# A three-stage mLSTM, mixture-of-experts and PReLU kernel: branch tables around whole experts replaced by straight code over 256 slots and one branch for the rest

## The chip, the cores and the metric

One NeuronCore of a Trainium2 chip runs the whole program. The metric is the device time of one execution in microseconds; lower is better.

## The reference

What is computed, cut to the steps that matter here (the recurrent first stage is left as a call):

```python
x = mlstm(q, k, v, i_gate, f_gate, o_gate)            # 1536 tokens x 320
logits = x @ w_gate                                   # 8 experts
expert_idx = np.argmax(logits, axis=1)
...
for i in range(N):                                    # first come, first served, 384 slots an expert
    e = expert_idx[i]
    if counts[e] < capacity:
        disp[e, counts[e]] = x[i]
...
h = np.maximum(np.einsum('ecd,edf->ecf', disp, w1), 0.0)   # 320 -> 1024
y = np.einsum('ecf,efd->ecd', h, w2)                       # 1024 -> 320
out[i] = gate_w[i] * y[expert_idx[i], pos[i]]
...
h = out @ w_in                                        # 320 -> 2048
g = np.maximum(h, 0.0) + alpha * np.minimum(h, 0.0)
return g @ w_out                                      # 2048 -> 320
```

How many tokens an expert gets depends on the data. With the seeded inputs the counts of experts 0 to 7 are 250, 143, 283, 182, 88, 227, 58 and 305.

## The kernel before, in words

**Three stages.** The mLSTM stage works through 12 blocks of 128 tokens, routes them and scatters each token's row into its expert's slots in DRAM (`disp`, 384 slots an expert). The expert stage takes the eight experts one after the other. The last stage (PReLU) gathers the tokens' rows back in groups of 2, 4, 4 and 2 blocks of 128 and runs 320 -> 2048 -> 320 over each group.

**Numbers as two halves.** Every matmul operand is a pair, high and low part in fp32r. ScalarE (ACT) copies a value to its high part, and VectorE (DVE) or GpSimd (POOL) subtracts the high part to get the low one (`less`, L183). A product is three matmuls: high by high, high by low, low by high. The inner dimension 320 is two blocks of 128 rows and one of 64; for the block of 64 the weight tile holds the high rows in its upper half and the low rows in its lower half, so that two matmuls do: one of 128 rows against the high part of x stored twice, and one of 64 rows against the low part of x (`layer1`, L926 to L937). One `layer1` call is eight matmuls. `layer2` (L944) is three matmuls of 320 columns for each block of 128 slots.

**An expert.** Its hidden dimension of 1024 is taken in eight steps f of 128. Step f does `layer1`, then the relu and its two parts (ACT L1082, DVE L1083), then `layer2` for step f - 2 (`LAG`). Beside it the weights of the next expert are split, a quarter (two steps) at a time, by `split1` and `split2`: the high parts on ACT, the low part of `w2` on POOL, that of `w1` on DVE except for the last quarter, which is POOL's; the next expert's rows are transposed and split (`expert_x`); and a piece of the last stage's float64 weights is converted on DVE with its parts on ACT and POOL (`split_f64`, five operations a piece; `CUT` says how many in each expert). Split weights live in a ring of six quarters (`ring1`, `ring2`), raw quarters in one set of buffers (`raw1`, `raw2`) that is loaded anew for each expert.

**The branch.** Each expert is emitted once for each number of slots (128, 256, 320 or 384) and for each number of blocks of the next expert: twelve arms, four for the last. `values_load` (L1163) reads the arm's number from `armi` into a register of PE, ACT, DVE and POOL, and `tc.Switch` (L1180) jumps into the arm; at its end each engine jumps back. With the counts above the slots computed are 256, 256, 320, 256, 128, 256, 128 and 320. SyncE (SP) issues the DMAs and takes no part in the switch.

**Order.** The instructions of PE, ACT, DVE and POOL stay in the order in which the code is written; SP's order is the scheduler's. The loads of expert e + 1 (`load_quarter`) stand ahead of the switch of expert e.

Of the kernel before, what the change touches and what calls it, by code (L numbers as in the profile page):

```python
# [53 lines left out]
def kernel(  # L54
# [39 lines left out]
    ARMS = [n for n in (P, 2 * P, 5 * P // 2) if n < SL] + [SL]  # L94

    W1, W2, W6, V7, V8, V9, G0, G1, NA, WA, WB, Z0, Z1, X0, LD, FL, XE, SC, SC0, L0, F0, WC, LS, UO, DL, LOV, XG, XG2, LV, L9, E0, S0, CUT, PQ = 12, 4, 0, 0, (1, 2, 1, 4, 1, 2, 0, 4, 2, 2, 2, 2, 1, 2, 4, 1), (1, 3, 4, 6), 2, 11, 6, 0, 6, 3, 6, 3, 3, (2, 1, 2, 4, 1), 5, (0, 1, 0, 1, 0, 1, 0, 3), (0, 0, 0, 0, 2, 0, 0, 1), 3, {5:[0], 6:[1], 7:[2]}, 0, 1, 1, 4, (12, ), (9, 11, 13), (11, 12, 13), 3, 3, 2, 0, (5, 5, 10, 5, 5, 5, 5, 20), ((3, ), (3, ))
# [39 lines left out]
    def x_tiles(pool, n, i):  # L136
        return [[pool.tile([P, n], F32R, name=f"x{i}{k}{x}", bufs=1) for x in "hl"] for k in range(3)]
# [4 lines left out]
    RING = 6  # L142
# [30 lines left out]
    def load_quarter(e, q, anchor=None):  # L173
        ds = [nc.sync.dma_start(out=raw_quarter(q)[:, :2], in_=w1[e, q])]
        if q % 2 == 0:
            ds.append(nc.sync.dma_start(out=raw1[q // 2][:r, 2, :], in_=w1t[e, :, q * QF:(q + 2) * QF]))
        ds.append(nc.sync.dma_start(out=raw2[q], in_=w2[e, :, 2 * q:2 * q + 2, :]))
        for d in ds:
            if anchor is not None:
                after(d, anchor)  # L180
# [42 lines left out]
    with ExitStack() as actx:  # L223
# [659 lines left out]
        arm, blks = (cp.tile([P, E], F32, name=nm) for nm in ("arm", "blks"))  # L883
        for t, ns in ((blks, range(P, SL, P)), (arm, ARMS[:-1])):
            for n in ns:
                if n == ns[0]:
                    nc.vector.tensor_single_scalar(out=t, in_=cps, scalar=float(n), op=ALU.is_gt)
                else:
                    nc.vector.scalar_tensor_tensor(out=t, in0=cps, scalar=float(n), in1=t, op0=ALU.is_gt, op1=ALU.add)
        nc.vector.scalar_tensor_tensor(  # L890
            out=arm[:, :E - 1], in0=blks[:, 1:], scalar=float(len(ARMS)), in1=arm[:, :E - 1], op0=ALU.mult, op1=ALU.add,
        )
# [33 lines left out]
    def layer1(ps, wh, wl, xp, fs, ks=(0, 2, 1)):  # L926

        n = ps.shape[-1]
        seq = []
        for k in ks:  # L930
            hi, lo = (t[:, :n] for t in xp[k])
# [21 lines left out]
    NRAW = 3  # L953
# [55 lines left out]
    def out_parts(q):  # L1009

        at = lambda i: (NQ * E + i) % RING
        if q in (2, 3):
            return [view(t, 2, DM) for t in ring1[at(q - 2)]]
        return ring2[at(q if q < 2 else q - 2)]
# [23 lines left out]
    ghl = [[mp.tile([P, SL], F32R, name=f"g{x}{i}") for x in "hl"] for i in range(LAG + 1)]  # L1038
# [9 lines left out]
    def expert_x(e, k, nblk):  # L1048
        x_part(lambda m: xd[:, m, :], nblk, lambda k: xps[k % 2], xp2[e % 2], k)
# [4 lines left out]
    def expert(e, n, nxt):  # L1054

        nblk = -(-n // P)

        def second(f, ms=range(nblk)):
            h2, l2 = ring2[(NQ * e + f // 2) % RING]
            gh, gl = (t[:, :n] for t in ghl[f % (LAG + 1)])  # L1060
            layer2([(m, accs[m]) for m in ms], gh, gl, h2[:, f % 2, :], l2[:, f % 2, :], f == 0, f == NF - 1)

        more = e + 1 < E
        shifts[:] = over
# [6 lines left out]
        per = len(steps) // NF  # L1071
        for f in range(NF):
            q, fo = divmod(f, 2)
            bank = lambda f: hps[f % (3 if more else 2)][:, :n]
            ps = bank(f)
            l1 = lambda f: (bank(f), *first_parts(e, f // 2), xp2[e % 2], slice(f % 2 * P, (f % 2 + 1) * P))
            if e or f >= E0:
                layer1(*l1(f))
            elif f == 0:
                first_layers([l1(f) for f in range(E0)])  # L1080
            gh, gl = (t[:, :n] for t in ghl[f % (LAG + 1)])
            nc.scalar.activation(gh, ps, AF.Relu)  # L1082
            nc.vector.scalar_tensor_tensor(out=gl, in0=ps, scalar=0.0, in1=gh.bitcast(F32), op0=ALU.max, op1=ALU.subtract)  # L1083
            x0 = X0 if e == 0 else XE
            if more and x0 <= f < x0 + 3:
                expert_x(e + 1, f - x0, nxt)
# [5 lines left out]
            if f >= LAG:  # L1092
                second(f - LAG)
# [4 lines left out]
            if more:  # L1098
                (split2 if fo else split1)(e + 1, q, nc.vector if not fo and q not in (PQ[1] if n > P else PQ[0]) else nc.gpsimd)
# [5 lines left out]
        for f in range(NF - LAG, NF if more else 0):  # L1105
            second(f)
        if more:
            while steps:
                steps.pop(0)()
            for m in range(nblk):  # L1110
                copy = nc.scalar.copy if m % 2 else nc.vector.tensor_copy
                p = min(P, n - m * P)
                copy(ysb[:p, m, :], accs[m][:p, :DM])
            return

        def put(m):
            p = min(P, n - m * P)
            for k in range(3):
                for a in range(2):
                    x = yhl[m][:p, a, k * P:min((k + 1) * P, DM)]  # L1120
                    nc.tensor.matmul(
                        fx[k][:x.shape[-1]], x, spot[:p, m, :GB0 * P], start=False, stop=m == nblk - 1 and a == 1,
                    )

        for m in range(nblk):
            for f in range(NF - LAG, NF):
                second(f, [m])
            p = min(P, n - m * P)
            hi, lo = (yhl[m][:p, a] for a in range(2))
            nc.scalar.copy(hi, accs[m][:p, :DM])  # L1130
            less(lo, accs[m][:p, :DM], hi, nc.vector)
            nc.gpsimd.tensor_tensor(out=ysb[:p, m, :], in0=hi.bitcast(F32), in1=lo.bitcast(F32), op=ALU.add)
        for m in range(nblk):
            put(m)
        while steps:
            steps.pop(0)()

# [4 lines left out]
    y_out = []  # L1142
# [7 lines left out]
    low_rows()  # L1150
    for e in range(E):
        if e == 3:
            last_steps()
        if e + 1 < E:
            x_in = load_x(e + 1)
            for q in range(NQ):
                load_quarter(e + 1, q, x_first if e == 0 else None)
        done = sum(CUT[:e]) // 5
        while loaded < min(done + NRAW, LD + done if e == 0 else 99):
            load_conv(loaded, x_in if e == 0 else None)  # L1160
            loaded += 1
        arms = len(ARMS) * (NBLK if e + 1 < E else 1)
        arm = nc.values_load(  # L1163
            armi[0:1, e:e + 1], engines=engines, min_val=0, max_val=arms - 1,
            skip_runtime_bounds_check_because="a count of comparisons",
        )
        over = list(shifts)
        if e == E - 2:
            nc.vector.tensor_copy(first_slots, gidx[:, :GB0].unsqueeze(2).to_broadcast([P, GB0, P]))
        if e == E - 1:  # L1170
            raw1 = raw2 = None
            yhl = [rw.tile([P, 2, DM], F32R, tag=f"w2r{m}", name=f"yhl{m}") for m in range(NBLK)]
            load_conv(loaded, raw=rw.tile([P, 3 * QF * 2], U32, tag="w1r1", name="raw"))
            loaded += 1
            spot = rw.tile([P, 3, 2 * QF], F32R, tag="w1r0", name="spot")
            nc.gpsimd.memset(xd[:, :GB0, :], 0.0)
# [58 lines left out]
    for gi, (i0, nb) in enumerate(PARTS):  # L1235
# [3 lines left out]
        for f in range(NFF):  # L1239
# [25 lines left out]
            def l2step(i0=i0, nb=nb, f=f, gh=gh, gl=gl, accs=accs):  # L1265
# [5 lines left out]
                if f == NFF - 1:  # L1271
                    osb = sp.tile([P, GB, DM], F32, tag="osb", name="osb", bufs=1)
                    for m in range(nb):
                        i = i0 + m

                        if m % 2:
                            nc.scalar.activation(osb[:, m, :], accs[m][:, :DM], AF.Copy, scale=gwt[:, i:i + 1])  # L1277
                        else:
                            nc.vector.tensor_scalar_mul(osb[:, m, :], accs[m][:, :DM], gwt[:, i:i + 1])
                        nc.sync.dma_start(out=out[i * P:(i + 1) * P, :], in_=osb[:, m, :])  # L1280
# [84 lines left out]
```

## Time and profile before

| what | value |
|---|---|
| median of 3 runs | 586.05 us (573.05 to 588.75) |
| profiled execution, its own time | 577.92 us |
| its span, first to last instruction | 576.1 us |
| mean granted TensorE clock | 0.855 of 2.4 GHz |
| PE busy, share of the span | 510.4 us, 89% |
| DVE, ACT, POOL busy | 299.6, 236.1, 224.5 us |

The stages follow one another: the mLSTM stage to about 126 us, the experts to about 366, the last stage to the end. Busy time is an average over stages with different limits; what an edit is worth is read from its own stage. A granted clock of 0.50 means 1.2 GHz, 1.00 means 2.4 GHz.

### The profile page before, as it was taken

The page shows a single profiled execution, that of the slowest core. Times are in us where ns is not written, and L with a number is a line of the kernel's source. Part 1 is how long each engine was busy: PE and PEld are TensorE (multiplying, and loading weights), DVE is VectorE, ACT ScalarE, POOL GpSimd, SP SyncE. Part 2 cuts the span into 40 slices and gives each one's busy share as a digit, 9 for nine tenths or more (in the row PEclk, how much of TensorE's full clock was granted, in tenths as well). Part 3 has the DMA queues.
Part 4 walks back from the last instruction along what each step waited for, and adds up shares of the span by engine and source line. Part 5 has one row for each costly group of instructions (what it writes and reads, how often), then busy time and mean ns, then how long its engine had stood idle before and what let it go on. Part 6 is the DMA issues. An engine that isn't in the chain of part 4 may idle for free. (4 is left out here: it accounts for less than half of the span.)

```text
span 576.1 us, 7915 instructions
## 1 busy us (share of the span) xinstructions
PE 510.4 (89%) x2699; PEld 425.5 (74%) x2699; DVE 299.6 (52%) x606; ACT 236.1 (41%) x563; POOL 224.5 (39%) x194
## 2 busy tenths in 40 slices
PE   7789988888787896969696969999999999999997
PEld 3578867866676674859575958788777877778886
DVE  8457636776748393927192639699221322122222
ACT  3467743343433242424242322355443434434443
POOL 3253344563423241414251442476453334232331
PEclk8779877576969896965595579999999999999999
DMA  7999994238956445454545053230010002000100
GB/s 216 271 281 334 324 279 159 68 105 245 246 148 178 128 140 173 141 166 134 173 132 176 0 153 92 85 92 0 24 46 1 1 0 71 0 1 1 47 1 23
DMA packets 41128, 69.91 MB, mean 121 GB/s; under 512 B 3999, under 2 KB 29922, under 8 KB 40975
## 3 DMA queue, kind: packets, MB, share of 16 engines
q1 hardware_dynamic: 39615, 64.18, 37.7%
q0 software_dynamic: 1152, 3.86, 2.1%
q8 instruction: 46, 0.75, 0.6%
q14 instruction: 107, 0.88, 0.6%
q10 hardware_dynamic: 208, 0.24, 0.1%
HBM read 56.49 MB, written 11.85 MB: 119 GB/s over the span
## 5 line engine op out<-in xcount | busy, mean ns | idle before, releaser
L183 POOL TENSOR_TENSOR g3l<-g,g3h 128x512 fp32r<-128x512 f32 (+1 forms) x61 | 66.7, 1094 | 112.4 <-ACT g3h L1258 112.3
L1255 DVE SCALAR_TENSOR_TENSOR g<-ng,nalt,g 128x256 f32<-128x256 f32 (+1 forms) x64 | 43.2, 675 | 124.8 <-ACT g L1254 122.9
L183 POOL TENSOR_TENSOR w2l<-w2r,w2h 128x640 fp32r<-128x640 f32 x31 | 53.4, 1721 | 116.8 <-ACT w2h L215 57.8
L1253 ACT ACTIVATE ng<-hps 128x256 f32<-128x256 f32 (+1 forms) x64 | 31.5, 493 | 102.8 <-PE hps L937 100.1
L1082 ACT ACTIVATE gh<-hps 128x256 fp32r<-128x256 f32 (+2 forms) x50 | 18.8, 375 | 116.5 <-PE qs L937 56.1
L1083 DVE SCALAR_TENSOR_TENSOR gl<-hps,gh 128x256 fp32r<-128x256 f32 (+2 forms) x50 | 20.4, 408 | 76.4 <-ACT gh L1082 72.9
L949 PE MATMUL acc<-w2h,gh 128*128 128x320 f32 (+1 forms) x128 | 46.0, 360 | 1.7 <-ACT gh L1082 1.7
L951 PE MATMUL acc<-w2h,gl 128*128 128x320 f32 (+1 forms) x128 | 43.6, 341 | 3.1 <-DVE gl L1083 3.1
L950 PE MATMUL acc<-w2l,g3h 128*128 128x320 f32 x144 | 44.5, 309 | 0.0
L951 PE MATMUL acc<-w2h,g3l 128*128 128x320 f32 x144 | 44.5, 309 | 0.0
L949 PE MATMUL acc<-w2h,g3h 128*128 128x320 f32 x144 | 44.4, 308 | 0.0
L950 PE MATMUL acc<-w2l,gh 128*128 128x320 f32 (+1 forms) x128 | 42.7, 334 | 0.0
L378 ACT ACTIVATE Gb<-Gb,bT 128x128 f32<-128x128 f32 x96 | 29.6, 390 | 14.0 <-POOL Gb L370 14.0
L1258 ACT CAST g3h<-g 128x256 fp32r<-128x256 f32 (+1 forms) x64 | 32.9, 515 | 0.3 <-DVE g L1255 0.3
L1254 ACT ACTIVATE g<-hps 128x256 f32<-128x256 f32 (+1 forms) x64 | 31.1, 486 | 1.6 <-POOL g3l L183 1.3
L384 PE MATMUL qs<-qbd,qk 120*128 120x384 f32 (+1 forms) x72 | 30.7, 573 | 0.4 <-DVE Pt L400 0.3
L951 PEld LDWEIGHTS acc<-w2h,gl 128*128 128x128 f32 (+1 forms) x128 | 26.0, 203 | 5.4 <-DVE gl L1083 5.2
L949 PEld LDWEIGHTS acc<-w2h,gh 128*128 128x128 f32 (+1 forms) x128 | 26.5, 207 | 2.5 <-ACT gh L1082 2.2
L949 PEld LDWEIGHTS acc<-w2h,g3h 128*128 128x128 f32 x144 | 27.1, 188 | 1.1
L950 PEld LDWEIGHTS acc<-w2l,g3h 128*128 128x128 f32 x144 | 27.0, 188 | 1.0
L447 PEld LDWEIGHTS Ops<-tk,Pt 128*128 128x128 f32 x192 | 26.4, 215 | 1.4 <-DVE Um L434 0.9
L937 PE MATMUL hps<-x10h,w1h 128*128 128x256 f32 (+1 forms) x26 | 9.5, 364 | 20.0 <-issue 19.3
(306 smaller groups left out, 1399.5 us busy)
## 6 DMA issues: line engine op xcount, KB each, us to landing
w2r<-w SPq DMA_DIRECT2D x32, 320.0 KB
w1r<-w SPq DMA_DIRECT2D x32, 256.0 KB
Gb<-gd SPq DMA_DIRECT2D x12, 512.0 KB
raw<-wout SPq DMA_DIRECT2D x8, 640.0 KB
raw<-win SPq DMA_DIRECT2D x8, 512.0 KB
tk<-tok SPq DMA_DIRECT2D x6, 648.0 KB
disp<-zt SPq DMA_DIRECT2D x4, 960.0 KB
yd<-held_rows SPq DMA_DIRECT2D x8, 480.0 KB
```

What stands on the lines that cost most here:

```text
L183: eng.tensor_tensor(out=out, in0=a, in1=b.bitcast(F32), op=ALU.subtract)
L378: nc.scalar.activation(Dt[i][:, h, :], Dt[i][:, h, :], AF.Exp, bias=bT[:, c, b * H + h:b * H + h + 1])
L384: nc.tensor.matmul(ps[:, :nh * P].rearrange("p (h t) -> p h t", h=nh), kst[:nh * D, g, :], qbd[:nh * D, h0:h0 + nh, :], start=True, stop=True,
L447: nc.tensor.matmul(Opss[i][:, h, :], Pts[i][:, h, :], v1t[:, h, :], start=True, stop=True)
L949: nc.tensor.matmul(a, gh[:, ms], wh, start=first, stop=False)
L950: nc.tensor.matmul(a, gh[:, ms], wl, start=False, stop=False)
L951: nc.tensor.matmul(a, gl[:, ms], wh, start=False, stop=last)
L1083: nc.vector.scalar_tensor_tensor(out=gl, in0=ps, scalar=0.0, in1=gh.bitcast(F32), op0=ALU.max, op1=ALU.subtract)
L1253: nc.scalar.activation(ng, ps, AF.Relu, scale=-1.0)
L1254: nc.scalar.activation(g, ps, AF.Relu)
L1255: nc.vector.scalar_tensor_tensor(out=g, in0=ng, scalar=nalt[:, f:f + 1], in1=g, op0=ALU.mult, op1=ALU.add)
L1258: nc.scalar.copy(gh, g)
```

## The change

The experts are no longer emitted in arms. Each is written once, in straight code over 256 slots (`N0`, two blocks), and behind it stands one `tc.If` with the third block of 128 slots (`rest_of`), which runs where an expert has more than 256 tokens (experts 2 and 7 here) and is jumped over elsewhere. POOL takes no part in the branch any more. The ring grows from six to eight quarters. The load of a quarter of expert e + 2 is written behind the subtraction of the low part of that quarter of expert e + 1, and the 64-row block of `w1` is loaded by quarters too. All low parts of weights go to POOL. The low part of x gets zeros in its lower 64 rows, and its matmul takes 128 rows. The next expert's x is always transposed for three blocks. Conversions are dealt out anew: eleven pieces before the last stage (two in expert 6, three in expert 7), where there were twelve, with two raw buffers for three. The outputs go through `held_rows`.

```diff
-    RING = 6
+    RING = 2 * NQ
...
+        t = [[pool.tile([P, n], F32R, name=f"x{i}{k}{x}", bufs=1) for x in "hl"] for k in range(3)]
+
+        nc.gpsimd.memset(t[2][1][r:].bitcast(U32), 0)
+        return t
...
-        if q % 2 == 0:
-            ds.append(nc.sync.dma_start(out=raw1[q // 2][:r, 2, :], in_=w1t[e, :, q * QF:(q + 2) * QF]))
+            nc.sync.dma_start(out=raw_quarter(q)[:r, 2, :], in_=w1t[e, :, q * QF:(q + 1) * QF]),
...
-                seq += [(wh[:, 2, fs], hi), (wh[:r, 2, fs], lo[:r])]
+                seq += [(wh[:, 2, fs], hi), (wh[:, 2, fs], lo)]
...
-    NRAW = 3
+    NRAW = 2
...
             if more:
-                (split2 if fo else split1)(e + 1, q, nc.vector if not fo and q not in (PQ[1] if n > P else PQ[0]) else nc.gpsimd)
+                (split2 if fo else split1)(e + 1, q, nc.gpsimd)
+                if fo and e + 2 < E:
+                    low_rows()
+                    load_quarter(e + 2, q)
...
+    def rest_of(e):
+
+        n = SL - N0
+        more = e + 1 < E
+        ms = range(NBLK - B0)
+
+        hb = xps if more else hps[:2]
+        for f in range(NF + LAG):
+            if f < NF:
+                ps = hb[f % len(hb)][:, :n]
+                layer1(ps, *first_args(e, f), c0=N0)
+                relu_parts(f, ps, n, N0)
+            if f >= LAG:
+                second(e, f - LAG, n, ms, N0)
...
-        arm = nc.values_load(
-            armi[0:1, e:e + 1], engines=engines, min_val=0, max_val=arms - 1,
...
-        for x in tc.Switch({g: arm for g in engines}, arms):
-            expert(e, ARMS[x % len(ARMS)], x // len(ARMS) + 1)
-
-        y_out.append(nc.sync.dma_start(out=y_rows(e), in_=ysb))
+        expert(e)
+
+        y_out.append(nc.sync.dma_start(out=y_rows(e)[:, :B0], in_=ysb[:, :B0]))
+        if B0 < NBLK:
+            more_slots = nc.values_load(
+                armi[0:1, e:e + 1], engines=engines, min_val=0, max_val=1,
...
+            with tc.If(more_slots != 0):
+                rest_of(e)
+            y_out.append(nc.sync.dma_start(out=y_rows(e)[:, B0:], in_=ysb[:, B0:]))
```

On PE, at the end of one expert and the start of the next, before (here expert 1 and the first arm of expert 1's switch; eleven more arms follow it):

```order
L949 MATMUL acc_1410<-w2h_105,gh_1402 128x320
L950 MATMUL acc_1410<-w2l_1374,gh_1402 128x320
L951 MATMUL acc_1410<-w2h_105,gl_1403 128x320
L1361 UNCONDITIONAL_BRANCH
L1163 TENSOR_LOAD armi
L1361 SWITCH_STRIDE
L1361 ISA x2
L1180 BRANCH_PREFETCH_HINT
L937 MATMUL hps_1406<-x10h,w1h_1369 128x128
L937 MATMUL hps_1406<-x10l,w1h_1369 128x128
```

Of this, the load of the arm's number and the jump into a table of arms go. The same engine now, at the end of expert 3 (`acc` the accumulators, `qs` the bank of the third block):

```order
L946 MATMUL acc_1420<-w2h_1373,gh_1407 128x320
L947 MATMUL acc_1420<-w2l_1383,gh_1407 128x320
L948 MATMUL acc_1420<-w2h_1373,gl_1408 128x320
L1203 TENSOR_LOAD armi
L1207 COMPARE_AND_BRANCH
L934 MATMUL qs_70<-x10h,w1h_1366 128x128
L934 MATMUL qs_70<-x10l,w1h_1366 128x128
```

88 matmuls of the third block follow the comparison, and behind them, on the same engine, stands the next expert:

```order
L946 MATMUL acc_1421<-w2h_1373,goh_1413 128x320
L947 MATMUL acc_1421<-w2l_1383,goh_1413 128x320
L948 MATMUL acc_1421<-w2h_1373,gol_1414 128x320
L1207 UNCONDITIONAL_BRANCH x2
L934 MATMUL hps_1417<-x00h,w1h_99 128x256
L934 MATMUL hps_1417<-x00l,w1h_99 128x256
```

A jump over the third block lands there, where a jump into an arm used to lie among twelve bodies.

On POOL, one arm of an expert before (`w1l` and `w2l` low parts of the next expert's weights, `winl` that of a converted piece):

```order
L183 TENSOR_TENSOR w2l_111<-w2r_94,w2h_103 128x640
L183 TENSOR_TENSOR w2l_1374<-w2r_95,w2h_105 128x640
L183 TENSOR_TENSOR w2l_1376<-w2r_96,w2h_1370 128x640
L183 TENSOR_TENSOR w1l_1377<-w1r_93,w1h_1371 128x512
L183 TENSOR_TENSOR w2l_1378<-w2r_97,w2h_1372 128x640
L183 TENSOR_TENSOR winl<-cv_1383,winh 128x2x256
L1361 UNCONDITIONAL_BRANCH
```

The same engine in one expert now, between two block ends:

```order
L188 TENSOR_TENSOR w1l_107<-w1r_93,w1h_99 128x512
L188 TENSOR_TENSOR w2l_108<-w2r_95,w2h_100 128x640
L188 TENSOR_TENSOR w1l_109<-w1r_93,w1h_101 128x512
L188 TENSOR_TENSOR w2l_110<-w2r_96,w2h_102 128x640
L188 TENSOR_TENSOR w1l_111<-w1r_94,w1h_103 128x512
L188 TENSOR_TENSOR winl<-cv_1387,winh 128x2x256
L188 TENSOR_TENSOR w2l_112<-w2r_97,w2h_104 128x640
L188 TENSOR_TENSOR w1l_1374<-w1r_94,w1h_105 128x512
L188 TENSOR_TENSOR w2l_1375<-w2r_98,w2h_106 128x640
L1207 UNCONDITIONAL_BRANCH
```

Three subtractions of `w1` have come over from DVE, and POOL's share of an expert goes from six to nine operations.

## Rows read from the trace of the kernel before

**Rows 1.** The page, granted TensorE clock in 40 equal slices of the span.

```profile
PEclk8779877576969896965595579999999999999999
```

**Rows 2.** Windows: stretch; length, busy time of each engine, granted clock, DMA share, GB/s.

```profile
249.50:280.00 30.50, 24.95 (x95) 22.46 (x96) 13.55 (x26) 9.35 (x20) 10.73 (x6) 0.50 0.53 158
280.00:308.00 28.00, 21.68 (x115) 18.25 (x114) 17.18 (x27) 9.88 (x21) 9.26 (x6) 0.80 0.47 141
...
338.00:368.00 30.00, 29.00 (x166) 24.41 (x166) 21.95 (x35) 7.41 (x15) 11.45 (x10) 0.94 0.30 89
368.00:403.00 35.00, 33.95 (x213) 29.27 (x214) 31.08 (x44) 19.82 (x54) 21.60 (x22) 1.00 0.18 53
...
450.00:500.00 50.00, 50.00 (x258) 39.97 (x257) 12.51 (x18) 22.30 (x44) 18.17 (x14) 1.00 0.06 21
```

**Rows 3.** Source: sequencer instructions of the branches; ns min/median/max, first and last start.

```profile
L1163 PEldq TENSOR_LOAD <-armi x8: 305/310/498, 125.3 to 331.5; - x8
...
L1180 PEldq BRANCH_PREFETCH_HINT  x8: 36/36/50, 131.0 to 338.0; - x8
...
L1361 PEldq COMPARE_BRANCH  x16: 311/2598/5832, 126.2 to 366.4; - x16
...
L1361 SPq COMPARE_BRANCH  x8: 33/33/38, 141.4 to 336.8; - x8
```

**Rows 4.** Timeline around the change from the fourth to the fifth expert, PE and ACT.

```profile
244.66 0.31 PE L951 MATMUL acc<-w2h,gl 128*128 128x320 f32 x1
...
249.54 0.36 PE L937 MATMUL hps<-x00h,w1h 128*128 128x128 f32 x1 [4.57 <-issue]
...
256.16 0.28 ACT L1082 ACTIVATE gh<-hps 128x128 fp32r<-128x128 f32 x1 [9.10 <-PE qs L937]
```

**Rows 5.** Timeline of PE, one layer-1 block of eight matmuls, 256 columns, last stage.

```profile
387.03 0.28 PE L937 MATMUL hps<-x00h,winh 128*128 128x256 f32 x1
387.15 0.28 PE L937 MATMUL hps<-x00l,winh 128*128 128x256 f32 x1
...
387.38 0.28 PE L937 MATMUL hps<-x02h,winh 128*128 128x256 f32 x1
387.59 0.38 PE L937 MATMUL hps<-x02l,winh 64*128 64x256 f32 x1
387.90 0.38 PE L937 MATMUL hps<-x01h,winh 128*128 128x256 f32 x1
388.12 0.28 PE L937 MATMUL hps<-x01l,winh 128*128 128x256 f32 x1
388.24 0.28 PE L937 MATMUL hps<-x01h,winl 128*128 128x256 f32 x1
```

**Rows 6.** The chain that ended last: start, us, what.

```profile
370.31 4.93 PE hps L937 x28
...
388.52 0.15 PE acc L949
...
389.40 0.44 PE xtp L923 x4
...
443.25 2.25 PE hps L937 x8
447.27 2.25 PE hps L937 x8
```

**Rows 7.** Source: low parts on DVE, 125 to 133 us; ns min/median/max, first and last start.

```profile
L183 DVE TENSOR_TENSOR w2l<-w2r,w2h x1: 6575/6575/6575, 125.7 to 125.7; 128x640 fp32r<-128x640 f32 x1
```

**Rows 8.** Groups by form on DVE and POOL, 187 to 340; busy us, mean ns | idle before.

```profile
L183 DVE TENSOR_TENSOR w1l<-w1r,w1h 128x512 fp32r<-128x512 f32 x15 | 15.0, 998 | 1.2 <-ACT w1h L202 1.2
...
L183 POOL TENSOR_TENSOR w2l<-w2r,w2h 128x640 fp32r<-128x640 f32 x20 | 35.9, 1797 | 85.3 <-ACT w2h L215 39.3 <-PE acc L950 32.6 <-PE hps L937 13.5
L183 POOL TENSOR_TENSOR winl<-cv,winh 128x512 fp32r<-128x512 f32 x6 | 7.8, 1298 | 9.2 <-ACT winh L202 9.2
L183 POOL TENSOR_TENSOR w1l<-w1r,w1h 128x512 fp32r<-128x512 f32 x5 | 6.8, 1366 | 4.5 <-ACT w1h L202 2.7 <-PE hps L937 0.8 <-DMA w2r<-w 0.7
```

More of the change, by code (lines that the diff above doesn't have):

```diff
@@ L882 @@
         scatter(len(todo))
[L883 to L892, printed above, removed]
+        arm = cp.tile([P, E], F32, name="arm")
+        nc.vector.tensor_single_scalar(out=arm, in_=cps, scalar=float(N0), op=ALU.is_gt)
         nc.vector.tensor_copy(armi, arm)
@@ L1070, in expert @@
             steps.append(now)
-        per = len(steps) // NF
+        per = -(-len(steps) // NF)
+        hb = banks(e)
         for f in range(NF):
             q, fo = divmod(f, 2)
-            bank = lambda f: hps[f % (3 if more else 2)][:, :n]
-            ps = bank(f)
-            l1 = lambda f: (bank(f), *first_parts(e, f // 2), xp2[e % 2], slice(f % 2 * P, (f % 2 + 1) * P))
+            ps = hb[f % len(hb)][:, :n]
             if e or f >= E0:
-                layer1(*l1(f))
+                layer1(ps, *first_args(e, f))
             elif f == 0:
[L1080 to L1083, printed above, removed]
+                first_layers([(hb[i % len(hb)][:, :n], *first_args(e, i)) for i in range(E0)])
+            relu_parts(f, ps, n)
             x0 = X0 if e == 0 else XE
             if more and x0 <= f < x0 + 3:
-                expert_x(e + 1, f - x0, nxt)
+                expert_x(e + 1, f - x0)
+                if f == x0 + 2 and e + 2 < E:
+                    x_in[0] = load_x(e + 2)
             if not more and f in SPOT:
@@ L1092, in expert @@
             if f >= LAG:
-                second(f - LAG)
+                second(e, f - LAG, n, range(B0))
             for k in F0.get(f, ()) if not more else ():
@@ L1104, in expert @@
                     steps.pop(0)()
-        for f in range(NF - LAG, NF if more else 0):
-            second(f)
         if more:
[L1108 to L1113, printed above, removed]
-            return
[L1116 to L1125, printed above, removed]
-            for f in range(NF - LAG, NF):
[L1127 to L1134, printed above, removed]
+            for f in range(NF - LAG, NF):
+                second(e, f, n, range(B0))
+            low_rows()
+            assert not steps
+            for m in range(B0):
+                (nc.scalar.copy if m % 2 else nc.vector.tensor_copy)(ysb[:, m, :], accs[m][:, :DM])
+            return
+        for m in range(B0):
+            for f in range(NF - LAG, NF):
+                second(e, f, n, [m])
+            own_rows(m)
         while steps:
             steps.pop(0)()
+    def rest_of(e):
[5 more added lines that the diff above has]
+            if f < NF:
+                ps = hb[f % len(hb)][:, :n]
+                layer1(ps, *first_args(e, f), c0=N0)
+                relu_parts(f, ps, n, N0)
+            if f >= LAG:
+                second(e, f - LAG, n, ms, N0)
+        for m in range(B0, NBLK):
+            if more:
+                nc.scalar.copy(ysb[:, m, :], accs[m][:, :DM])
+            else:
+                own_rows(m, nc.vector)
     def zero_raw():
@@ L1150 @@
     low_rows()
+    engines = [mybir.EngineType.PE, mybir.EngineType.Activation, mybir.EngineType.DVE]
     for e in range(E):
```

88 lines of the change are left out of this document (54 added, 34 removed).

## The prediction

> **What bounds the kernel now.** I read the page's clock row first, then the windows by expert, then the branch instructions, then PE's timeline, then the chain. TensorE's clock is full from the 25th slice to the end and ragged before [rows 1]. The expert stage is where it is lost: the expert with 128 slots (249.5 to 280) ran wholly at 1.2 GHz, the next one, with 256 slots, at a mean of 0.80 [rows 2]. From the prefetch hint of the first expert (131.0) to that of the last (338.0) there are seven experts [rows 3], 29.6 us each, whatever their size: 30.5 us for 128 slots, 28.0 for 256 [rows 2].
>
> Why size buys nothing stands at an arm's start. PE's last matmul of an expert starts at 244.66, its first of the next at 249.54, 4.57 us of idle time that no engine's work ended ("issue"), and ACT, which must jump too, begins at 256.16 [rows 4]. In between lies the switch's compare-and-branch on PE: sixteen of them, median 2.6 us, longest 5.83 us [rows 3]; each expert has a short one out of its arm (311 ns is the shortest) and a long one into the next. After the gap PE works at half clock.
>
> The last stage is PE's: 50.00 busy of 50 us at full clock [rows 2], and the chain there is PE alone, a step of 512 columns every 4.02 us (443.25 to 447.27), of which `layer1` takes 2.25 [rows 6]. In `layer1` one matmul breaks the pace. Starts are 0.12 us apart (387.03, 387.15), but around the 64-row one they are 0.21 (387.38 to 387.59), 0.31 (to 387.90) and 0.22 (to 388.12), then 0.12 again [rows 5]. The three cost 0.74 where 0.35 would do: 0.39 us in each of 128 blocks of eight, 64 in experts and 64 in the last stage.
>
> **The change part by part.** The sum is made against the profiled execution, 577.9 us, which lies 1.4% under the median of the runs shown; I leave the result on that footing.
>
> *The 64-row matmul.* It becomes a 128-row one. A block of 256 columns goes from 1.33 to 8 x 0.117 = 0.94 us; for 512 columns, 2.25 to 8 x 0.235 = 1.88, by twice the 256-column pitch. I take 0.39 for both. Of the last stage's 64 blocks, 48 lie in its three later groups, where PE is the bound [rows 2, 6]: 18.7 us off. The first group (368 to 403) has DVE busy 31.1 of 35 us and POOL 21.6 [rows 2], and it now gets five conversions instead of four. Its 16 blocks would save 6.2 us, a fifth conversion could cost up to a quarter of that group, 8.8 us; I take nothing. The Trainium skill, page "TensorE: Matmul & The Clock Gate", section "Why this matters for your kernels", says that a matmul with a short contraction takes as long as one over 128 rows; by it this edit would save nothing. No row here has a 64-row matmul that runs at the common pace, so the row decides for me, and the rule gets a chance below.
>
> *The switch goes, a branch comes.* Removed per expert: the long jump. Added: a load of the register (305 to 498 ns on PE [rows 3]), a compare-and-branch, and a wait until the engine's own work is done before it passes. PE's sequencer runs ahead of its matmuls, so the load and the compare hide behind the queue; the drain doesn't. Queued behind it is the next expert's first `layer1`; ACT's and DVE's own branch stands after their copy of the last accumulators, and PE has three `layer1` blocks, 2.8 us, before it needs them. Price of the jump: SP's branch to code right behind it took 33 ns, a jump into a far arm up to 5.83 us [rows 3]. Both ends stay; the third block is short and the target lies right behind it, so I take the near one: 0.8 us of PE for each expert.
>
> The Trainium skill, "Runtime: NRT & Kernel Launch", section "Instruction fetch mechanics", says that a taken branch stalls for a fetch when its target is outside a window of two pages of 256 instructions. 88 matmuls with their weight loads are 176 instructions, so by it the jump mostly stays inside; that no row shows such a jump on PE, ACT or DVE is why the other price has a rival of its own.
>
> *A straight expert.* PE: 8 x 0.94 `layer1`, 8 x 6 x 0.147 `layer2` (388.52 to 389.40 is six [rows 6]), nine transposes at 0.11 (four in 0.44 [rows 6]), 0.8 for the branch: 7.5 + 7.1 + 1.0 + 0.8 = 16.4 us at full clock, which should hold as the long gap goes. But POOL now subtracts all: 4 x 1.80 + 4 x 1.37 + 1.30 = 14.0 us [rows 8], and DVE falls from 17.2 [rows 2] by three operations of 1.0 [rows 8] to 14.2. The two don't run freely beside each other: a subtraction on DVE stood for 6.58 us at 125.7 [rows 7]. In the busiest stretch, 368 to 403, DVE and POOL together were busy 52.7 in 35 us [rows 2], 1.5 us per us. At that rate 28.2 us of work take 18.8. The ends are 16.4 (free beside each other) and 28.2 (one after the other); I take 19, by the nearest row. ACT (about 12) and DMA (4.2 MB, at 141 GB/s for a share of 0.47 [rows 2] some 14 us) stay below; the earlier load and the wider ring therefore only keep raw quarters off the path and are counted at nothing. If that cover went, a late quarter would show as ACT waiting for a DMA. The four quarter loads of the 64-row part add DMAs to SP, which issues for well under half of an expert.
>
> *The third block.* Experts 2 and 7 go from 320 to 384 slots, and the extra 128 run alone behind the rest: 8 x (8 x 0.11 + 3 x 0.147) = 10.6 us at full clock. A stretch of 128 columns ran at 1.2 GHz throughout [rows 2], which would make it 21. I take 16. Experts 4 and 6 go from 128 to 256 slots, which is in the 19 us.
>
> *The sum.* Before, from 131.0 [rows 3] to the last stage's first chained matmul at 370.3 [rows 6]: 239.3 us. After: expert 0, still started at half clock by the splitting of x, 22; four straight ones 76; expert 2, 35; expert 6 with a second conversion 23.5 (between 19 and 19 + 8.8); expert 7 16.5 + 16; combining and splitting 5. Together 194, so 45.3 less. With 18.7 in the last stage: 577.9 - 45.3 - 18.7 = **514 us**.
>
> **The rivals.**
>
> *The branch costs what the switch did.* Every engine then still jumps far. For: sixteen branches on PE with a median of 2.6 us [rows 3]. Against: SP's near jump. An expert is then the 28.0 of now less 8 x 0.39, about 25 us: 6 x 7 = 42 more, **556 us**. 15%.
>
> *DVE and POOL don't collide.* Then an expert is 16.4 and the third block stays at full clock: 514 - 5 x 2.6 - 2 x 5.4 = **490 us**. For: ACT and DVE work mostly from PSUM in the relu. Against: [rows 7]. 13%.
>
> *Short contractions cost the same* (the rule above). No saving in the last stage and 8 x 0.39 per expert, hidden mostly in the 19: **533 us**. 6%.
>
> *POOL shuts DVE out.* Place: `gl` stands on DVE behind the conversions, and PE's `layer2` waits for it. If POOL's nine operations run without gaps as at 125.7, an expert is the serial 28.2, PE falls to half clock in the waits, the third blocks take 21 each: experts 30 + 6 x 28.2 + 9 + 33 + 42 + 5 = 288, 49 more than before, less 19 in the last stage: **607 us**, slower. It decides from about 23.4 us an expert on. For: [rows 7]; against: POOL's operations wait for ACT's copies, one a step, so gaps remain (85 us of idle time before `w2l` [rows 8]). 4%.
>
> **How the numbers follow.** The forecast has 62%, the rivals 15, 13, 6 and 4. The range runs from the case without collisions to the dear branch, 488 to 556. Under 566 lie all cases but the last and a tail of the second: faster by over 2% (about what a measurement of this kernel can tell from no change) 0.93, within 2% 0.03, slower 0.04.
>
> **What would show it.** Right: gaps of PE at expert ends below 1.5 us; the granted clock at 1.00 through experts 3 to 5; starts of PE 0.12 us apart through a whole `layer1`; steps of 512 columns every 3.6 us; experts some 19 us apart; DVE operations of 0.5 us drawn out under POOL's. Wrong: "issue" gaps of 4 to 5 us on PE before each expert, `layer1` blocks still at 1.33, ACT waiting for `w1r` or `w2r`, or the first group of the last stage longer than 37 us.

## The result and the profile after

The changed kernel takes 518.32 us, median of four runs (515.6 to 519.07), against 582.68 for four runs of the kernel before: a ratio of 0.899, 95% interval 0.889 to 0.909. The forecast was 514, within 488 to 556. The profiled execution took 518.73 us, its span is 517.0.

The clock row, [rows 1] before, has lost its half-speed slices in the expert stage; the ragged part in front of it, the mLSTM stage, stays.

```profile
PEclk9869796858979999999988999988999999999899
```

The windows that answer to [rows 2], with the same columns: expert 2's third block, one straight expert from first relu to first relu, expert 7's third block, and most of the last stage's first group.

```profile
189.30:200.05 10.75, 10.75 (x90) 10.75 (x90) 3.75 (x20) 2.64 (x9) 0.40 (x1) 1.00 0.14 50
219.85:239.65 19.80, 16.91 (x123) 15.69 (x122) 16.53 (x23) 10.47 (x22) 14.17 (x9) 1.00 0.75 216
306.00:316.50 10.50, 10.50 (x88) 10.50 (x88) 2.65 (x10) 2.64 (x9) 1.10 (x2) 1.00 0.01 2
320.00:360.00 40.00, 35.21 (x229) 32.58 (x228) 32.89 (x46) 21.04 (x57) 23.41 (x23) 0.91 0.22 67
```

A straight expert takes 19.80 us at full clock, where the two experts of [rows 2] took 28.0 and 30.5. The third blocks are TensorE alone, without a gap. In the first group the clock fell to 0.91.

The branches now, as [rows 3], min, median and max of their ns; ten rather than eight because the third block, where it runs, ends in a jump of its own.

```profile
L1207 PEldq COMPARE_BRANCH  x10: 68/216/357, 147.1 to 315.1; - x10
L1207 DVEq COMPARE_BRANCH  x10: 47/56/72, 147.8 to 316.9; - x10
L1207 ACTq COMPARE_BRANCH  x10: 38/45/50, 148.5 to 315.9; - x10
```

TensorE's timeline at the change from expert 3 to expert 4, which answers to [rows 4]:

```profile
218.16 0.31 PE L948 MATMUL acc<-w2h,gl 128*128 128x320 f32 x1
218.62 0.36 PE L934 MATMUL hps<-x00h,w1h 128*128 128x256 f32 x1
```

The next expert starts 0.46 us after the last matmul of the one before began; it was 4.88. And a `layer1` block of 512 columns, which answers to [rows 5]: starts are 0.23 us apart through the block of 64 too (`x32`).

```profile
394.46 0.40 PE L934 MATMUL hps<-x32h,winh 128*128 128x512 f32 x1
394.69 0.39 PE L934 MATMUL hps<-x32l,winh 128*128 128x512 f32 x1
394.92 0.39 PE L934 MATMUL hps<-x31h,winh 128*128 128x512 f32 x1
395.15 0.39 PE L934 MATMUL hps<-x31l,winh 128*128 128x512 f32 x1
```

By the forecast's own steps, all from the two profiled executions:

| step | forecast | measured |
|---|---|---|
| expert 0 | 22 | 23.7 |
| straight experts 1, 3, 4, 5 | 19 each | 19.8 each |
| expert 2 with its third block | 19 + 16 | 19.3 + 10.8 |
| expert 6, two conversions | 23.5 | 26.5 |
| expert 7, combine and split | 37.5 | 34.7 |
| expert stage, to the last stage's first chained matmul (370.3 before, 319.7 now) | 194, was 239.3 | 195.6 |
| last stage's later groups | -18.7 | -12.9 |
| last stage's first group | 0 | +4.3 |
| start of the expert stage (131.0 before, 124.1 now) | 0 | -6.9 |

For the last stage I use two marks on ACT: from its first relu to the second one of 512 columns ("first group": 39.0 us before, 43.3 after), and from there to the last relu ("later groups": 158.6 before, 145.7 after).

### The profile page after: what moved, and what is told of

The parts are those of the page before. It is cut to its first block, busy times and chain, and to the rows that moved or that the text cites. A ratio compares the mean times of both kernels' runs of the same rounds, so it can differ in the third digit from the quotient of the medians.

```text
span 517.0 us, 8262 instructions
## 1 busy us (share of the span) xinstructions
PE 459.1 (89%) x2896; PEld 411.9 (80%) x2896; DVE 304.3 (59%) x596; ACT 242.6 (47%) x582; POOL 256.1 (50%) x218
## 5 line engine op out<-in xcount | busy, mean ns | idle before, releaser
L188 POOL TENSOR_TENSOR w1l<-w1r,w1h 128x512 fp32r<-128x512 f32 x31 | 46.9, 1512 | 21.4 <-ACT w1h L207 21.2
L948 PE MATMUL acc<-w2h,gl 128*128 128x320 f32 x128 | 43.3, 339 | 15.0 <-DVE gl L1058 14.5
L946 PE MATMUL acc<-w2h,gh 128*128 128x320 f32 x128 | 42.2, 330 | 0.0
L948 PEld LDWEIGHTS acc<-w2h,gl 128*128 128x128 f32 x128 | 25.0, 196 | 20.7 <-DVE gl L1058 20.7
L947 PE MATMUL acc<-w2l,gh 128*128 128x320 f32 x128 | 40.7, 318 | 0.0
L947 PE MATMUL acc<-w1l,g3h 128*128 128x320 f32 x96 | 30.1, 313 | 1.2 <-POOL w1l L188 1.2
L948 PE MATMUL acc<-w1h,g3l 128*128 128x320 f32 x96 | 30.2, 315 | 0.4 <-POOL g3l L188 0.3
L946 PE MATMUL acc<-w1h,g3h 128*128 128x320 f32 x96 | 30.3, 315 | 0.0
L1057 ACT ACTIVATE gh<-hps 128x256 fp32r<-128x256 f32 x50 | 19.2, 384 | 22.4 <-PE hps L934 20.7
L1058 DVE SCALAR_TENSOR_TENSOR gl<-hps,gh 128x256 fp32r<-128x256 f32 x50 | 20.8, 418 | 13.4 <-ACT gh L1057 12.9
```

The costliest lines, as they stand in the source:

```text
L188: eng.tensor_tensor(out=out, in0=a, in1=b.bitcast(F32), op=ALU.subtract)
L946: nc.tensor.matmul(a, gh[:, ms], wh, start=first, stop=False)
L947: nc.tensor.matmul(a, gh[:, ms], wl, start=False, stop=False)
L948: nc.tensor.matmul(a, gl[:, ms], wh, start=False, stop=last)
```

## The experiments

Where the table has no other note, a kernel is the changed one with the edit shown. In the last three columns are the two marks of the last stage and a straight expert (expert 4; with `l_two`, where two experts met a dear jump, one that didn't). The kernel before, timed beside these runs, had medians from 576.6 to 582.7 us, so medians of different rows compare to about 1%; smaller differences are read from the traces.

| run | median, us | straight expert | first group | later groups |
|---|---|---|---|---|
| before | 582.7 | 29.4, mean of 1 to 6 | 39.0 | 158.6 |
| after | 518.3 | 19.8 | 43.3 | 145.7 |
| a_short | 542.4 | 20.2 | 43.2 | 158.6 |
| b_full, on before | 549.9 | 28.4, mean of 1 to 6 | 39.0 | 140.9 |
| c_slot | 515.0 | 19.8 | 42.9 | 140.9 |
| d_never | 498.6 | 19.8 | 43.3 | 145.7 |
| e_long, on d_never | 526.8 | 23.9 | 42.1 | 145.8 |
| l_two, on d_never | 508.7 | 19.8 | 42.2 | 142.7 |
| f_w1dve | 522.2 | 20.7 | 42.2 | 144.6 |
| g_two | 501.8 | 17.7 | 43.2 | 142.4 |
| h_four | 517.2 | 19.8 | 42.3 | 142.4 |
| i_act | 505.2 | 18.3 | 41.9 | 143.7 |
| j_gl | 516.8 | 19.8 | 40.8 | 144.1 |
| k_best | 501.4 | 18.3 | 40.5 | 140.9 |

### The 64-row matmul: a_short and b_full

```diff
-                seq += [(wh[:, 2, fs], hi), (wh[:, 2, fs], lo)]
+                seq += [(wh[:, 2, fs], hi), (wh[:r, 2, fs], lo[:r])]
```

> The changed kernel (518.3 us) with one edit undone: the low part of x goes through the block of 64 with 64 rows again. Theory (the forecast's): a 64-row matmul among 128-row ones costs 0.37 to 0.42 us in every layer-1 block where TensorE sets the pace, so the 48 blocks of the last stage's later groups take 4.0 us a step again instead of 3.6 and that part gives back 18 to 20 us, the third blocks of experts 2 and 7 some 3 us each, and the straight experts, which wait for DVE at 19.8 us and have 16.9 us of TensorE in them, at most 1 us each: 540 to 550 us. Rival (rows of the contraction cost nothing, the gain of the last stage came with the buffers or the outputs): 516 to 521 us, steps of 3.6 us.

Measured 542.39 us, ratio to before 0.943 (0.936 to 0.950). The pace breaks at the same place as in [rows 5], in this run's timeline of a block of 512 columns:

```profile
403.18 0.40 PE L934 MATMUL hps<-x32h,winh 128*128 128x512 f32 x1
403.51 0.50 PE L934 MATMUL hps<-x32l,winh 64*128 64x512 f32 x1
403.94 0.50 PE L934 MATMUL hps<-x31h,winh 128*128 128x512 f32 x1
404.28 0.40 PE L934 MATMUL hps<-x31l,winh 128*128 128x512 f32 x1
```

0.33, 0.43 and 0.34 where the rows after have 0.23 each: 0.41 us. A step is 4.01 us again. The third block of expert 2 took 13.2 us (2.4 more), a straight expert 0.4 more, and TensorE is then busy 19.6 of its 20.2 us. The later groups gave back 12.9, not 18 to 20; why, the slot shows below.

The other way round, the edit alone on the kernel before:

```diff
-                seq += [(wh[:, 2, fs], hi), (wh[:r, 2, fs], lo[:r])]
+                seq += [(wh[:, 2, fs], hi), (wh[:, 2, fs], lo)]
...
+        nc.gpsimd.memset(t[2][1][r:].bitcast(U32), 0)
```

> The kernel before (about 580 us) with this edit alone: zeros in the lower 64 rows of the low part of x and a matmul of 128 rows. Theory: the later groups of the last stage fall from 4.0 to 3.6 us a step (16 to 20 us), its first group from 2.2 to 1.8 us a step where TensorE sets it (up to 6 us), and the experts, where TensorE was busy for most of each, by 0.4 us for each of 64 blocks at most (up to 25 us, of which DVE and POOL let through about a third): 540 to 562 us. Rival (the edit pays only beside the straight experts): 575 us or more.

Measured 549.95 us, 0.956 (0.949 to 0.964) of before: about 27 us from two lines. The later groups lost 17.7 us (forecast 18.7); an expert about 1 of the 3.1 us that its eight blocks could save; the first group nothing. Windows of this run, first group and later:

```profile
359.00:394.00 35.00, 32.49 (x218) 31.16 (x217) 31.02 (x41) 19.31 (x54) 23.57 (x21) 0.90 0.13 38
410.00:450.00 40.00, 40.00 (x228) 36.20 (x227) 10.53 (x15) 18.36 (x36) 16.90 (x13) 1.00 0.04 12
```

The rival that the number of rows costs nothing is out.

### The outputs' slots: c_slot

What the forecast didn't count: "the outputs go through `held_rows`" puts four blocks of a group into three slots, so the fourth shares the first one's. ACT's timeline after, at the end of the third group:

```profile
480.79 0.53 ACT L1305 ACTIVATE held_rows<-acc,gwt 128x320 f32<-128x320 f32 x1
485.71 0.53 ACT L1305 ACTIVATE held_rows<-acc,gwt 128x320 f32<-128x320 f32 x1 [4.39 <-DMA out<-held_rows]
486.13 0.38 ACT L1281 ACTIVATE ng<-hps 128x256 f32<-128x256 f32 x1
```

ACT stands 4.39 us until the transfer of the first block is out, and the next group's relu stands behind it. At the end of the second group it had stood 2.47 us for the same reason (426.79). The edit gives the fourth block a place of its own:

```diff
-                        osb = held_rows[:, i % (NTB - OB), :]
+                        osb = held_rows[:, m, :] if m < NTB - OB else raw64[0][:, :DM].bitcast(F32)
```

> The changed kernel with the outputs of the last stage's groups of four blocks in four places (the fourth block in a raw buffer that is free by then) instead of three slots of held_rows, where the fourth block's slot is the first block's and ACT stood 2.5 us at 424 and 4.4 us at 481 for the transfer out of it. Theory: both waits go; the first was mostly made good by the queue of finished layer-1 blocks behind it (about 1 us lost), the second cost 4 to 5 us with the half clock after it: 512 to 514 us. Rival (ACT has slack enough there and another wait takes the place): 517 us or more.

Measured 514.99 us, 0.894 (0.887 to 0.901). That is just above what the theory had; the medians differ by 3.3 us and the runs overlap, but the trace is plain. The same place in this run:

```profile
480.72 0.53 ACT L1305 ACTIVATE held_rows<-acc,gwt 128x320 f32<-128x320 f32 x1
481.60 0.53 ACT L1305 ACTIVATE raw<-acc,gwt 128x320 f32<-128x320 f32 x1 [0.35 <-PE acc L948]
482.55 0.38 ACT L1281 ACTIVATE ng<-hps 128x256 f32<-128x256 f32 x1 [0.43 <-PE hps L934]
```

The later groups take 140.9 us, as in `b_full`, where outputs had four places. So the 128-row matmul is worth 17.7 us there and the shared slot took 4.9 back. In other runs with that slot the later groups took 142.4 to 145.8: the wait's price varies with the transfer. In `a_short` ACT stood 2.4 us at the third group's end and the stretch is no longer than before's: with the slower TensorE the wait was hidden, so undoing the edit showed only 12.9.

### The third block and the jumps: d_never, e_long, l_two

```diff
-        nc.vector.tensor_single_scalar(out=arm, in_=cps, scalar=float(N0), op=ALU.is_gt)
+        nc.vector.tensor_single_scalar(out=arm, in_=cps, scalar=float(NS), op=ALU.is_gt)
```

> The changed kernel with a threshold that no expert reaches, so that all eight jumps are taken and the slots beyond 256 of experts 2 and 7 are left out. Theory from the profile after: the two third blocks are 10.7 and 10.4 us long, all of it on the path, so 495 to 499 us, and experts 3 to 6 begin 10.5 us earlier with the same 19.8 us each. Rival (the forecast's 16 us for each block, because the next expert or the combine also starts better off): 484 to 488 us. Second rival (what a third block takes is given back by DVE and POOL, which catch up on weights and conversions beside it, so that expert 3 gets longer without it): 503 us or more.

Measured 498.62 us: 19.7 less, ratio 0.862 (0.855 to 0.869). The first theory: the two blocks cost nearly all of their 10.8 and 10.4 us, and no more. All eight jumps are now taken (no expert reaches the threshold `NS`), and cheap:

```profile
L1207 PEldq COMPARE_BRANCH  x8: 215/312/352, 149.0 to 295.9; - x8
```

Then more code between branch and target, three copies of the third block and two:

```diff
             with tc.If(more_slots != 0):
-                rest_of(e)
+                for _ in range(3):
+                    rest_of(e)
```

> The run with no third block (498.6 us) and the code that each jump passes made three times as long: 264 matmuls instead of 88 on TensorE. The slots beyond 256 of experts 2 and 7 are left out. Theory (a jump is cheap because its target lies near, within what has been fetched): now it costs what the switch's jumps did, 2.6 to 5.8 us on TensorE, less what hides, at each of eight places, and more where ACT and DVE come late: 511 to 535 us, with idle time put down to nothing before each expert's first matmul. Rival (it is cheap because it is a compare-and-branch and no table): 496 to 502 us, and compare-and-branch still under 0.4 us.

Measured 526.77 us, 28.2 more, ratio 0.911 (0.905 to 0.918). Nothing of the added code runs, yet every jump on TensorE is dear now, and it idles until the jump is done:

```profile
L1207 PEldq COMPARE_BRANCH  x8: 3380/3720/5419, 147.9 to 320.8; - x8
```

```profile
223.32 0.54 PE L934 MATMUL hps<-x00h,w1h 128*128 128x256 f32 x1 [3.38 <-PEq L1207]
```

> As the run with three copies of the code behind each branch, all passed over (526.8 us; 498.6 with one), but with two: 176 matmuls and their weight loads to pass on TensorE. The slots beyond 256 of experts 2 and 7 are left out. By the Trainium skill, Runtime: NRT & Kernel Launch, Instruction fetch mechanics, two pages of 256 instructions are at hand, so a jump over 352 is mostly still inside: 498 to 506 us. Rival (the price grows with the distance): half way, 510 to 516 us. Second rival (what counts is whether the target had been fetched when the branch came, and one copy was already the most): 522 to 528 us.

Measured 508.74 us, 10.1 more than with one copy, ratio 0.883 (0.877 to 0.890):

```profile
L1207 PEldq COMPARE_BRANCH  x8: 312/329/5037, 146.0 to 305.0; - x8
```

Neither a growing price nor all alike: of the eight jumps two were dear (5.04 and 4.85 us, at 188.1 and 254.2), six stayed at 0.3. But not all of the six were free. Behind three of them, 0.7 to 1.9 us after the jump had ended, TensorE stood still in straight code with no engine to wait for: 2.78, 3.02 and 2.27 us of idle time, before 172.14, 237.45 and 308.31. Neither `d_never` nor `e_long` has such a stretch.

```profile
172.14 0.28 PE L934 MATMUL hps<-x02l,w1h 128*128 128x256 f32 x1 [2.78 <-issue]
```

What TensorE waits for is code, by the traces: the DMA queue that moves instructions (`q8 instruction`, some 16 KB a transfer) has one transfer in each of these five stretches of `l_two` and one in each of the eight jumps of `e_long`, where it starts 0.9 to 2.5 us into the jump; it has none in the eight jumps of `d_never`. For the jump at 188.1, window 188.0 to 193.2:

```profile
q8 instruction: 1, 0.02, 1.2%
```

So a jump is cheap when its target has been loaded, and whether it has depends on where the code lies. My numbers for the theory were too low (498 to 506): "mostly still inside" is two misses of eight, and three more stops just behind a hit. The Trainium skill's rule (Runtime: NRT & Kernel Launch, Instruction fetch mechanics; a window of two pages of 256 instructions) agrees with all three runs' jumps: 176 instructions to pass, no dear jump; 352, two of eight; 528, all eight. That section's other figure, room for 2048 instructions on TensorE, doesn't: by it none would have been dear. DVE's and ACT's jumps, over far fewer instructions, stayed under 0.08 us in all three.

### What sets the straight expert: f_w1dve, g_two, i_act

TensorE's waits in three experts after, 200 to 260 us, say DVE (us in total, times, longest):

```profile
PE acc L948 <- DVE gl L1058: 3.6, 6, 0.7
PE qs L920 <- DVE x00l L188: 2.9, 2, 1.4
PE qs L920 <- DVE x10l L188: 1.4, 1, 1.4
PE hps L934 <- PEq L1207: 0.2, 1, 0.2
```

DVE and POOL beside each other, from the timelines of expert 4 ([rows 7, 8] before):

```profile
221.44 1.53 DVE L972 TENSOR_SCALAR cv<-raw 128x768 uint32<-128x768 uint32 x1
223.00 1.80 DVE L973 TENSOR_SCALAR cv<-cv 128x768 f32<-128x768 f32 x1
224.73 0.41 DVE L1058 SCALAR_TENSOR_TENSOR gl<-hps,gh 128x256 fp32r<-128x256 f32 x1
...
225.53 0.82 DVE L975 TENSOR_SCALAR cv<-cv 128x768 uint32<-128x768 uint32 x1
```

```profile
221.03 1.52 POOL L188 TENSOR_TENSOR w1l<-w1r,w1h 128x512 fp32r<-128x512 f32 x1 [1.27 <-ACT w1h L207]
222.51 1.88 POOL L188 TENSOR_TENSOR w2l<-w2r,w2h 128x640 fp32r<-128x640 f32 x1
224.35 1.58 POOL L188 TENSOR_TENSOR w1l<-w1r,w1h 128x512 fp32r<-128x512 f32 x1
```

L972 takes 1.53 us, L973 1.80, L975 0.82, and each ends 0.41 or 0.42 us after the POOL operation beside it (that one at its start plus its length: 222.55, 224.39, 225.93). `gl`, which reads one operand from PSUM, takes its 0.41 in the middle of POOL's 1.58. With POOL idle when it starts, as in expert 4 of `f_w1dve` below, the same L972 takes 0.56 us:

```profile
223.88 0.56 DVE L972 TENSOR_SCALAR cv<-raw 128x768 uint32<-128x768 uint32 x1
```

The Trainium skill (SBUF — State Buffer, SBUF: two separate sides) has DVE and POOL take turns at one pair of ports, each for a whole instruction, where DVE's operation has two SBUF inputs or runs in a mode that uses two ports; the ends of the three rows agree, and whether these operations, of one input each, run in such a mode no row here shows. Is the 19.8 the sum of both engines' work, as the forecast reckoned, or DVE's alone? First, three quarters of `w1`'s low parts go back to DVE:

```diff
-                (split2 if fo else split1)(e + 1, q, nc.gpsimd)
+                (split2 if fo else split1)(e + 1, q, nc.vector if not fo and q < 3 else nc.gpsimd)
```

> The changed kernel (518.3 us) with the low parts of w1 of three quarters back on DVE (1.0 us each there, 1.4 to 1.5 on POOL), as before. Theory (the straight expert's 19.8 us is what DVE and POOL need beside each other, 1.5 us of work in each us): POOL loses 4.5 us of work, DVE gains 3, the sum falls by 1.5 and the expert by up to 1 us or stays: 19 to 20 us, 510 to 520 us in all. Rival (DVE alone sets the 19.8 us, drawn out by POOL): DVE gains 3 us and more, experts of 21.5 to 23 us, 530 to 545 us.

Measured 522.18 us, 0.907 (0.898 to 0.916). An expert of this run:

```profile
221.60:242.30 20.70, 17.41 (x123) 15.66 (x122) 17.79 (x26) 10.44 (x22) 9.53 (x6) 1.00 0.74 209
```

The sum of DVE and POOL fell from 30.7 to 27.3 us, and the expert still grew by 0.9. So the rate of 1.5 that carried the forecast is no law; what counts is DVE's own time, 16.5 before this edit and 17.8 with it. The rival overshot: DVE gained 1.3 us, not 3, as less of its work is drawn out.

Then two DVE operations of each conversion are left out:

```diff
-            lambda: ts(out=t, in0=t, scalar1=4, scalar2=1, ...
-            lambda: stt(out=z, in0=high, scalar=0x80000000, in1=t, ...
+            (lambda: None) if i < NCV else lambda: ts(out=t, in0=t, ...
+            (lambda: None) if i < NCV else lambda: stt(out=z, in0=high, ...
```

> The changed kernel (518.3 us) without two of the five DVE operations of each conversion in the experts, the shift and the one that sets the sign (the converted weights of the last stage are other numbers). Alone they take 0.5 and 0.8 us, under POOL's 1.74 each. Theory (DVE beside POOL sets the straight expert's 19.8 us): 17.3 to 18.6 us an expert, 6 to 16 us in all: 502 to 512 us. Rival (TensorE's 16.9 us and its drain at the branch set it): experts stay within 0.4 us, 515 to 519 us.

Measured 501.84 us, 0.871 (0.863 to 0.878):

```profile
213.10:230.80 17.70, 16.08 (x123) 15.65 (x122) 14.57 (x21) 10.64 (x22) 14.57 (x9) 1.00 0.87 242
```

2.0 us off DVE, 2.1 off the expert. (The two had been busy 3.0 us, 0.82 and 2.22.) Nothing is left out when two other operations move to ACT:

```diff
-            nc.vector.tensor_copy(parts[k][0][r:2 * r, :n], hi)
+            nc.scalar.copy(parts[k][0][r:2 * r, :n], hi.bitcast(F32))
...
-                (nc.scalar.copy if m % 2 else nc.vector.tensor_copy)(ysb[:, m, :], accs[m][:, :DM])
+                nc.scalar.copy(ysb[:, m, :], accs[m][:, :DM])
```

> The changed kernel (518.3 us) with two of DVE's operations on ACT: the copy of the first accumulator at an expert's end (0.49 us) and the copy of the 64 high rows of x into the upper half (0.42 us alone, 0.99 beside POOL). Nothing is left out. ACT is busy 10.5 of 19.8 us in a straight expert. Theory (DVE beside POOL sets the pace, as the run with two operations fewer showed with 2.1 us an expert for 1.3 to 3.3 us of work): 18.3 to 19.2 us an expert, 507 to 514 us in all. Rival (the two stand where DVE has time, the end of the expert and while TensorE waits for x, and ACT's second copy now ends later than DVE's did): 19.6 to 20.3 us an expert, 516 to 521 us.

Measured 505.22 us, 0.876 (0.866 to 0.887), 13 us better than the changed kernel and better than the theory had:

```profile
215.70:234.00 18.30, 16.35 (x123) 15.66 (x122) 15.02 (x21) 11.56 (x23) 14.94 (x9) 1.00 0.79 231
```

Over the four kernels expert 4 is DVE's busy time and 2.9 to 3.3 us more, and it doesn't follow POOL's (14.2, 9.5, 14.6 and 14.9). So DVE's work sets the pace, drawn out by POOL. It is DVE's work on the path that counts: expert 5 after has one more operation of 1.14 us on DVE at its end, where DVE has time, and takes 19.8 us all the same with DVE busy 17.6.

### The last stage's first group: h_four, j_gl

TensorE's waits there, after:

```profile
PE acc L948 <- POOL g3l L188: 2.4, 3, 1.8
PE xtp L920 <- DVE x30l L188: 2.2, 1, 2.2
PE acc L947 <- POOL w1l L188: 1.2, 1, 1.2
```

DVE's five operations of the first of five conversions are left out (`i == NCV`):

```diff
+        if i == NCV:
+            steps = [low_rows] + [lambda: None] * 3
```

> The changed kernel (518.3 us) with DVE's operations of the first of the last stage's five conversions left out (a part of w_out is another number there). From the last stage's first relu to the second one of 512 columns it is 43.3 us now and was 39.0 before. Theory (the fifth conversion is what ate the gain of the 128-row matmul in this group and 4 us more): 38 to 40 us, 513 to 515 us in all. Rival (POOL's low parts and gathers or the wait for raw weights, now in two buffers, set it): 42 to 44 us, 516 to 519 us.

Measured 517.24 us, 0.898 (0.890 to 0.905). The group took 42.3 us; in runs that leave it as it is it takes 42.1 to 43.3, so the theory is out: what DVE does for one conversion more isn't what the group pays for. Then POOL's part:

```diff
-eng=nc.vector if gi == len(PARTS) - 1 and f >= NFF - LV else nc.gpsimd
+eng=nc.vector if gi == len(PARTS) - 1 and f >= NFF - LV or gi == 0 and f < 6 else nc.gpsimd
```

> The changed kernel (518.3 us) with the first six low parts of the PReLU's values in the last stage's first group on DVE instead of POOL. Theory (in the first 15 us of this group the chain runs over POOL, its low parts of 0.8 us, four gathers of 1.0 to 1.4 and the conversions' low parts): the group, 43.3 us from the first relu to the second one of 512 columns, falls by 2 to 4 us, 514 to 517 us in all. Rival (DVE, busy 33.5 of 41 us there, sets it, and the operations are late for it): 43 to 46 us, 518 to 522 us.

Measured 516.84 us, 0.893 (0.882 to 0.905), by the medians no difference; in the trace the group is 40.8 us, 1.4 us under the shortest of those, and TensorE's waits for POOL's `g3l` are gone, though one for DVE's stands in their place:

```profile
PE xtp L920 <- DVE x30l L188: 2.1, 1, 2.1
PE acc L948 <- DVE g3l L188: 1.9, 1, 1.9
PE acc L947 <- POOL w1l L188: 1.2, 1, 1.2
```

So 1.4 to 2.5 of the 4.3 us that the group lost lie in POOL's queue, by one trace of a group that varies by 1.2 us. The rest stays open: the fifth conversion's part on POOL and ACT, and the two raw buffers in place of three, weren't tried apart.

### Together: k_best

`i_act`, `c_slot` and `j_gl` in one kernel.

> Three edits together on the changed kernel: the two operations moved from DVE to ACT (505.2 us alone), a place of its own for the fourth output block (515.0 alone; between the second relu of 512 columns and the last relu that run took 140.9 us, the run with the two operations moved 143.7) and the first six low parts of the last stage's first group on DVE (516.8 alone; that group took 40.8 us, 41.9 in the run with the two operations moved). Nothing is left out. Theory (they are in different stages and add, as far as a stage has not had it already): 505.2 - 2.8 - 1.1 to 505.2 - 2.8 - 2.5 = 500 to 501.5 us, experts of 18.3 us. Rival (with DVE's load in the first group up by six operations and the low parts of x waiting behind them, the third edit costs there): 503 to 506 us.

Measured 501.39 us (six runs, 499.73 to 504.93), 0.865 (0.860 to 0.870) of the kernel before, 3% below the changed kernel. The three add as far as expected (500 to 501.5). Behind expert 0 its clock row has one slice below 9:

```profile
PEclk9759995978989999999989999999999999999999
```

## Why the prediction was right

**The switch.** Right: the gap before an expert fell from 4.57 us to almost nothing, and the nearby target is the reason, as the step had it (0.8 us taken; the compare itself is 0.2 to 0.4). The rival with the dear branch was a real one: `e_long`, without third blocks, has dear jumps at every expert, and they cost 28 us, not the 42 given.

**The straight expert.** 19.8 for 19, but not for the reason given, so the hit is in part luck. "1.5 us per us" met the number; `f_w1dve` showed that the sum of two engines doesn't set it. DVE's time does, some of it spent waiting for POOL: the 14.2 us of work reckoned for DVE were busy for 16.5. Expert 6 with its second conversion was put 3 us too low (26.5 us, DVE busy 22.6 of it): TensorE waited for DVE twice there, 3.0 us each for `gl` and `x10l`, and its granted clock was 0.83 from 266 us on. Expert 0, forecast as "started at half clock", ran at 1.00 to 143 us and at 0.50 from 144 to 150, behind a wait of 3.15 us for DVE's `gl`.

**The third block.** Wrong term: 16 us each was the middle between full and half clock, but the low end, 10.6, was what came: 10.8 and 10.4. The slow 128-slot expert of [rows 2] had run behind a long gap; these run behind a busy expert, at a granted clock of 1.00. It was an average of two cases of which only one applied; 10.8 us of error on the safe side over the two.

**The 64-row matmul.** Right where TensorE is the bound: 17.7 us for 18.7. The Trainium skill's rule that a short contraction takes as long as a full one (TensorE: Matmul & The Clock Gate, Why this matters for your kernels) speaks of a single matmul and doesn't hold in this stream of matmuls: a 64-row one among 128-row ones costs 0.3 to 0.4 us a block.

**The last stage otherwise.** Two terms failed. "The outputs go through `held_rows`" was given no price and cost 4.9 us. "I take nothing" for the first group was within its bounds (-6.2 to +8.8) and became +4.3; of this the fifth conversion on DVE, which I had named, is not the cause. By the forecast's own mark, up to the first step of 512 columns, the group went from 35.0 to 38.7 us, so its sign of being wrong here (longer than 37 us) came.

**The start.** The expert stage began 6.9 us earlier (expert 0's first matmul at 124.1; the switch's hint at 131.0 before, [rows 3]). No switch stands in front of it any more, which the sum left out: before, TensorE stood 3.25 us between its last matmul of the mLSTM stage and expert 0's first (131.35), where there is no gap now. The other part is the mLSTM stage itself, whose last matmul ended at 128.1 before and at 124.3 after. In `b_full`, with the switch, it ended at 124.6, so that part is variation between runs: luck.

So the total came out near because errors cancelled: the third blocks 10.8 us and the start 6.9 better than reckoned, the last stage 10.1 and the rest of the expert stage about 12 worse (0.8 for each straight expert, 1.7 in expert 0, 3 in expert 6, 2.8 in expert 7 apart from its third block, the rest at the edges).

## What to carry to other kernels

Branch over little code: on TensorE a jump over 176 instructions cost 0.2 to 0.4 us, one over 528 cost 3.4 to 5.4 us and some of the clock behind it (0.93 in a straight expert); here straight code for the common size with the rest behind a short branch beat a table of whole arms though it computes more. Fill a contraction to the full 128 rows with zeros where its matmul stands among full ones and TensorE is the bound. Reckon DVE and POOL not by the sum of their work but by DVE's own time, drawn out by POOL, and move work from it to ACT; and where an edit sends outputs through another buffer, count its slots.

## What the runs showed of the hardware

A jump's price on TensorE went by place, not by distance alone: with two copies of the same code two jumps of eight cost 4.9 and 5.0 us and six 0.3, and behind three of the six TensorE stood 2.3 to 3.0 us in straight code. Each of these stretches has a transfer of instructions in it, and each of the eight jumps of 3.4 to 5.4 us over three copies. The 64-row matmul slows not itself alone but the two starts around it (0.33, 0.43 and 0.34 us for 0.23 at 512 columns), and by 0.41 us at 512 columns, 0.29 at 128, nearly the same whatever the width.
